# A reordered first ten microseconds: x tiles 4 and 5 load ahead of two weight remainders, x 1 on the sync queue, T2 one chunk earlier, and xT of tile 3 copied in halves

## The chip, the cores and the metric

One core of one Trainium2 chip. The metric is the device time of one execution in microseconds (us). Every execution told of here was in the fast state: the granted clock was 0.997 to 1.0 of full speed in all of them.

Positions such as "T2 at 7.38" are us from the first instruction of the profiled execution. PE is TensorE's matmul, PEld its weight load, DVE VectorE, ACT ScalarE, POOL GpSimd, SP SyncE (which issues most DMA loads). PSUM is the memory into which PE writes. T0, T1 and so on are the four transposes of that tile of x; K0, Q0, H4 and the like are accumulations of matmuls, each in one bank.

## The reference, cut to what matters

```python
x  = A_x                                  # [1, 2048, 448] bf16
xn = _layernorm(x, axis=-1)
s  = _A_ref(xn, A_wqkv, A_wo)             # linear attention: 16 heads of 28, phi(t) = t+1 or exp(t)
g  = _silu(_B_ref(xn, B_w1, B_b1, B_w2, B_b2))   # FFN 448 -> 1792 -> 448, squared ReLU
return x + s * g
```

Only the beginning matters: x is normalized per token (DVE), transposed (PE, via PSUM), and multiplied by wqkv and w1. 448 columns are three contraction chunks of 128 rows and a remainder of 64 rows.

## The kernel before

The program is written op by op in Python and put in order per engine; the first ~9 us, "the head", are laid out by hand. The loads go out in this order (cut):

```python
load_x(0, 1)
load_x(1, 2, "act").prio = -118                     # x tile 1: issued by ScalarE
twins = load_k("sp", w_qkv, A_wqkv, "wk", 384, 2 * D, later=True)   # "wk": the K part of wqkv
load_x(2, 4)
# ... b1 on ScalarE's queue ...
load_w1("w1a", 0, 512, 2, [twins])                  # two main loads, then twins, then the 64-row remainders
load_x(4, 8)
load_w1("w1b", 512, 1024)
load_k("sp", w_qkv, A_wqkv, "wq", 0, 384)
load_w1("w1c", 1024, F)
```

A DMA issued from SP occupies SP while it is issued, and SP issues one after the other. The last loads of `load_w1` are the 64-row remainders of w1 ("w1 rests" below for those of w1a).

A tile of x becomes normalized (`ln_norm`, columns 0 to 383), then its last 64 columns are written twice into columns 384 to 511 (`ln_last`, the "twin", so that 64-row matmuls can run in pairs on both halves of the array). Then four 128x128 transposes go into one PSUM bank and one copy takes them to xT:

```python
def pe_transpose(si, part, eng):
    b = Buf("T")                                    # a PSUM bank of its own
    chunks = range(4) if part is None else (2 * part, 2 * part + 1)
    # ... one transpose per chunk into b; the fourth reads the twin ("xd") ...
    if eng == "dve":
        return e.tensor_copy(dst, src)
    return e.activation(out=dst, in_=src, func=AF.Copy)
```

PE's order in the head (cut); `first` and `second` are the two token halves of the first four h (= w1) accumulations:

```python
turn(0, 0, "act"); turn(0, 1, "act"); turn(1, 0, "act")    # T0, first half of T1
mains(k0, (0,), ...); mains(k0, (1,), ...); mains(k0, (2,), ...)   # K of tile 0
turn(1, 1, "act")
mains(k1, (0, 1), ...); h_mains(0, (0, 1)); mains(k1, (2,), ...)
# ... b1 transpose ...
h_mains(0, (2,)); h_mains(1); h_mains(2)
head["xT2"] = pe_transpose(2, None, "act")                 # T2
h_mains(3)
head["xT3"] = pe_transpose(3, None, "dve")                 # T3
rests(k0, k1)                                              # 64-row remainders of K
rests(first[0], first[2]); rests(first[1], first[3])       # 64-row remainders of h: need the w1 rests
pe_four(*second)                                           # second halves of h: need xT of tiles 2 and 3
# then K2 H4 K3 H6, H5 Q0 Q1 H7 H8 ...                     # H4 on needs w1b, H8 on needs w1c
```

## Time and profile before

| | before |
|---|---|
| time, median of 3 (range) | 141.42 us (141.3 to 141.51) |
| span of the profiled execution | 139.7 us |
| PE busy | 136.6 us (98%) |
| T2 starts, second half of h starts, K2 starts | 7.38, 8.84, 10.38 us |
| landed: wk, x 2 and 3, w1 rests, last of w1b, last of w1c | 4.07, 4.73, 7.03, 10.51, 15.38 us |

From the page of the profile of before: the span, each engine's busy time, and by engine the chain of work that ended last.

```profile
span 139.7 us, 3106 instructions
...
PE 136.6 (98%) x1255; PEld 68.0 (49%) x1255; DVE 92.2 (66%) x226; ACT 77.8 (56%) x152; POOL 25.0 (18%) x33
...
PE 95%; DVE 2%; DMA 2%; issue 0%; DVEq 0%
```

TensorE is the limit nearly everywhere. So the change can only win or lose time in which PE stands still or runs slowly in the head. PE's timeline there (start, duration, engine, line, operation, out<-in, shapes, count; an idle time before it would follow in brackets):

```profile
4.92 0.81 PE L641 MATMUL pb<-w_qkv,xT 128*128 128x512 bf16 x3
...
6.60 0.93 PE L688 MATMUL pb<-xT,w 128*128 128x256 bf16 x7
7.38 0.40 PE L528 MATMUL pb<-ident,xn 128*128 128x128 bf16 x4
7.61 0.49 PE L688 MATMUL pb<-xT,w 128*128 128x256 bf16 x3
7.94 0.39 PE L528 MATMUL pb<-ident,xn 128*128 128x128 bf16 x4
8.26 0.39 PE L641 MATMUL pb<-w_qkv,xT 64*128 64x512 bf16 x2
8.48 1.30 PE L688 MATMUL pb<-xT,w 64*128 64x256 bf16 x18
...
10.38 1.03 PE L641 MATMUL pb<-w_qkv,xT 64*128 64x512 bf16 x8
```

The first line is K0, the last K2; the L528 lines are T2 and T3. The view merges both halves of h into the line of 8.48; the weight loads (PEld) show where the second half starts:

```profile
8.84 1.42 PEld L688 LDWEIGHTS pb<-xT,w 64*128 64x128 bf16 x28 [0.26 <-DVE xT L537]
```

A matmul's shown duration includes its latency, so compare starts: seven h matmuls fill 6.60 to 7.38, about 0.11 us each. DVE's timeline in the same execution:

```profile
5.10 0.62 DVE L463 BATCH_NORM_STATS2 st<-x_tok 128x6 f32<-128x448 bf16 x1
...
6.94 0.37 DVE L486 TENSOR_SCALAR xn<-x_tok,mv,rstd 128x384 bf16<-128x384 bf16 x1
7.26 0.31 DVE L512 TENSOR_SCALAR xn<-x_tok,mv,rstd 128x128 bf16<-128x128 bf16 x1
...
8.36 0.42 DVE L537 COPY xT<-pb 128x512 bf16<-128x512 bf16 x1 [0.49 <-PE pb L528]
```

The statistics of x 2 ("st2" below) start at 5.10 without a wait, as x 2 and 3 landed at 4.73. xn of tile 2 is done at 7.31, 0.07 before PE comes to T2. The copy of xT 3 ends at 8.78, and the second half of h starts right after it, at 8.84. And the loads as SP issues them (duration: of issuing, not of moving data):

```profile
0.44 0.42 SPq L401 DMA_DIRECT2D w_qkv<-in_A_wqkv_dram  x1
0.91 0.49 SPq L401 DMA_DIRECT2D x_tok<-in_A_x_dram  x1
...
3.68 1.24 SPq L401 DMA_DIRECT2D w<-in_B_w_dram  x2
4.96 0.59 SPq L401 DMA_DIRECT2D x_tok<-in_A_x_dram  x1
5.58 1.62 SPq L401 DMA_DIRECT2D w<-in_B_w_dram  x3
...
9.06 1.77 SPq L401 DMA_DIRECT2D w<-in_B_w_dram  x3
```

In this order: wk, x 2 and 3, the w1 rests, x 4 to 7, w1b, w1c. One issue takes 0.4 to 0.6 us, and SP is never idle.

### The profile page before, as it was taken

The page shows a single profiled execution, that of the slowest core. Times are in us where ns is not written, and L with a number is a line of the kernel's source. Part 1 is how long each engine was busy: PE and PEld are TensorE (multiplying, and loading weights), DVE is VectorE, ACT ScalarE, POOL GpSimd, SP SyncE. Part 2 cuts the span into 40 slices and gives each one's busy share as a digit, 9 for nine tenths or more (in the row PEclk, how much of TensorE's full clock was granted, in tenths as well). Part 3 has the DMA queues.
Part 4 walks back from the last instruction along what each step waited for, and adds up shares of the span by engine and source line. Part 5 has one row for each costly group of instructions (what it writes and reads, how often), then busy time and mean ns, then how long its engine had stood idle before and what let it go on. Part 6 is the DMA issues. An engine that isn't in the chain of part 4 may idle for free.

```text
span 139.7 us, 3106 instructions
## 1 busy us (share of the span) xinstructions
PE 136.6 (98%) x1255; PEld 68.0 (49%) x1255; DVE 92.2 (66%) x226; ACT 77.8 (56%) x152; POOL 25.0 (18%) x33
## 2 busy tenths in 40 slices
PE   9999999999999999999999999999999999999992
PEld 2474444444444444444455455645555555555481
DVE  3989899799878994889995900329636071542653
ACT  4769787879988878979788912422033030301220
POOL 6000000000000000000893000000002328091770
DMA  6997367999723200000000148960000103111122
GB/s 190 247 335 219 77 170 186 356 276 144 131 52 70 60 6 0 0 19 5 0 0 0 42 120 169 175 107 0 0 0 5 66 0 101 35 66 66 38 99 68
DMA packets 20354, 12.91 MB, mean 92 GB/s; under 512 B 9524, under 2 KB 19956, under 8 KB 20340
## 3 DMA queue, kind: packets, MB, share of 16 engines
q1 hardware_dynamic: 18332, 11.52, 33.3%
q10 hardware_dynamic: 2008, 1.20, 4.3%
q8 instruction: 10, 0.16, 0.5%
q14 instruction: 4, 0.03, 0.1%
HBM read 8.78 MB, written 2.10 MB: 78 GB/s over the span
## 4 chain that ended last, share of the span: by engine, by line
PE 95%; DVE 2%; DMA 2%; issue 0%; DVEq 0%
PE pb L955 31%; PE pb L688 30%; PE pb L641 9%; PE pb L1021 8%; PE pb L722 7%; PE pb L672 6%; DMA x_tok<-in_A_x_dram 2%; PE pb L528 1%; PE pb L728 1%; DVE st L463 1%; PE pb L815 1%; PE pb L776 1%; PE pb L853 0%; DVE xn L991 0%; DVE mv L464 0%; PE pb L846 0%
## 5 line engine op out<-in xcount | busy, mean ns | idle before, releaser
L688 PE MATMUL pb<-xT,w 64*128 64x512 bf16 (+2 forms) x408 | 51.6, 365 | 0.0
L955 PE MATMUL pb<-w,r 64*128 64x448 bf16 (+3 forms) x406 | 44.9, 343 | 0.0
L697 ACT ACTIVATE r<-pb,b1f 128x512 bf16<-128x512 f32 x56 | 35.1, 688 | 4.2 <-PE pb L688 4.2
L688 PEld LDWEIGHTS pb<-xT,w 64*128 64x128 bf16 (+1 forms) x408 | 22.8, 94 | 22.5 <-ACT r L697 0.5
L955 PEld LDWEIGHTS pb<-w,r 64*128 64x128 bf16 (+1 forms) x406 | 22.8, 95 | 19.9 <-issue 0.7
L966 DVE TENSOR_TENSOR gbuf<-pb,b2b 128x448 bf16<-128x448 f32 (+1 forms) x16 | 9.2, 608 | 30.0 <-PE pb L955 30.0
L931 ACT ACTIVATE gbuf<-gbuf 128x448 bf16<-128x448 bf16 (+1 forms) x16 | 8.7, 565 | 36.0 <-DVE gbuf L966 35.5
L1000 POOL TENSOR_TENSOR xn<-xn,x_tok 128x448 bf16<-128x448 bf16 x15 | 15.0, 1032 | 46.3 <-DVE xn L991 46.3
L641 PE MATMUL pb<-w_qkv,xT 64*128 64x512 bf16 (+1 forms) x106 | 17.8, 376 | 0.0
L672 PE MATMUL pb<-xT,w_qkv 64*128 64x512 bf16 x84 | 15.5, 376 | 0.0
L705 DVE TENSOR_TENSOR r<-r 128x512 bf16<-128x512 bf16 x42 | 14.4, 418 | 0.0
L390 POOL MEMSET kvm<- 128x2048 bf16 x1 | 1.8, 1804 | 63.4 <-DVE zb L666 63.4
L1021 PE MATMUL pb<-msb,pqT 64*128 64x448 bf16 (+3 forms) x93 | 10.9, 343 | 0.0
L629 DVE SCALAR_TENSOR_TENSOR qk<-pb,qk 128x512 bf16<-128x512 f32 x16 | 10.6, 685 | 0.2
L463 DVE BATCH_NORM_STATS2 st<-x_tok 128x6 f32<-128x448 bf16 x16 | 9.3, 610 | 2.0 <-DMA x_tok<-in_A_x_dram 2.0
L991 DVE TENSOR_TENSOR xn<-pb,gbuf 128x448 bf16<-128x448 f32 (+2 forms) x17 | 9.2, 591 | 2.0 <-ACT gbuf L931 1.5
L619 ACT ACTIVATE qk<-pb 128x512 bf16<-128x512 f32 x16 | 8.9, 593 | 3.0 <-PE pb L641 2.5
L641 PEld LDWEIGHTS pb<-w_qkv,xT 64*128 64x128 bf16 (+1 forms) x106 | 6.7, 94 | 6.0 <-ACT xT L538 0.2
L722 PE MATMUL pb<-qk,xn 128*128 128x448 bf16 x48 | 9.3, 353 | 0.0
L619 ACT ACTIVATE pqT<-pb 128x512 bf16<-128x512 f32 x12 | 6.8, 597 | 3.2 <-PE pb L688 1.6
L672 PEld LDWEIGHTS pb<-xT,w_qkv 64*128 64x128 bf16 x84 | 6.0, 94 | 5.0
L706 ACT ACTIVATE r<-r 128x512 bf16<-128x512 bf16 x14 | 8.4, 637 | 0.0
(71 smaller groups left out, 99.7 us busy)
## 6 DMA issues: line engine op xcount, KB each, us to landing
out_dram<-xn SPq DMA_DIRECT2D x15, 112.0 KB, 1.7
w<-in_B_w_dram SPq DMA_DIRECT2D x1, 1568.0 KB, 10.0
x_tok<-in_A_x_dram SPq DMA_DIRECT2D x3, 448.0 KB, 3.8
xT<-rows ACTq DMA_DIRECT2D x6, 112.0 KB
w<-in_B_w_dram SPq DMA_DIRECT2D x1, 576.0 KB, 4.6
xT<-rows SPq DMA_DIRECT2D x5, 112.0 KB
w_o<-in_A_wo_dram SPq DMA_DIRECT2D x1, 392.0 KB, 11.3
w_qkv<-in_A_wqkv_dram SPq DMA_DIRECT2D x1, 384.0 KB, 3.6
```

The costliest lines, as they stand in the source:

```text
L463: add("dve", lambda e, _: e.bn_stats(st6[:, si, :], x_tok[:, si, :]), [("x", si)], [("st", si)], 0.58),
L619: add("act", lambda e, _: e.activation(out=slot, in_=src(), func=AF.Exp), [buf, "actw"], [tile], 0.6)
L629: lambda e, _: e.scalar_tensor_tensor(out=slot, in0=src(), scalar=1.0 + 1e-6, in1=slot, op0=ALU.add, op1=ALU.max),
L641: return e.matmul(ps(b)[:, 0:512], xT[half[h], c, si * P : (si + 1) * P], w_qkv[half[h], c, 384 : 2 * D], start=start, stop=stop,)
L672: return e.matmul(ps(b)[:, 0:512], w_qkv[half[h], c, m * P : (m + 1) * P], xT[half[h], c, g * 512 : (g + 1) * 512], start=start, stop=stop,)
L688: return e.matmul(ps(b)[:, c0 : c0 + n], w_1[half[h], c, fi * P : (fi + 1) * P], xT[half[h], c, t : t + n], start=start, stop=stop,)
L697: lambda e, _: e.activation(out=slot, in_=ps(b)[:, 0:512], func=AF.Relu, bias=b1f[:, fi : fi + 1]),
L705: return e.tensor_tensor(out=slot, in0=slot, in1=slot, op=ALU.mult)
L722: last = e.matmul(ps(b)[:, 0:D], xn[:, si, c * P : (c + 1) * P], pk_of(si), start=(si == 0), stop=(si == NT - 1),)
L955: return e.matmul(ps(b)[:, 0:n], r2[half[h], fi, si * P : (si + 1) * P], w_2[half[h], fi, c], start=start, stop=stop)
L1000: eng, lambda e, _: e.tensor_tensor(out=ob, in0=ob, in1=x_tok[:, si, c], op=ALU.add),
L1021: return e.matmul(ps(b)[:, 0:n], q, m, start=start, stop=stop)
```

## The change

The intent: shorten the wait at 8.84 (both engines copy half of xT 3 at the same time), give x 4 and 5 to DVE earlier, free ScalarE's queue at the start, shorten the twin's write, and let T2 and K0 start sooner. The diff, cut to its core:

```diff
         load_x(0, 1)
-        load_x(1, 2, "act").prio = -118
+        load_x(1, 2)
 # ...
-        load_w1("w1a", 0, 512, 2, [twins])
-        load_x(4, 8)
+        load_w1("w1a", 0, 512, 2, [twins, lambda: load_x(4, 6)])
+        load_x(6, 8)
 # ... ln_norm: all 448 columns also for tiles 1 to 3 (was 384)
-            twin = head[f"xd{i}"] = ln_last(i)
+            twin = head[f"xd{i}"] = ln_twin(i, i + 1, "dve") if i else ln_last(i)
 # ...
         warm(8, wide=True)
+        warm(2)
 # ...
+        mains(k0, (0,), [("xT", 0, "a")] + wnames("wk")[:1])
         turn(1, 0, "act")
-        mains(k0, (0,), [("xT", 0, "a")] + wnames("wk")[:1])
 # ...
         h_mains(1)
+        head["xT2"] = pe_transpose(2, None, "act")
         h_mains(2)
-        head["xT2"] = pe_transpose(2, None, "act")
         h_mains(3)
-        head["xT3"] = pe_transpose(3, None, "dve")
+        turn(3, 0, "dve")
+        turn(3, 1, "act")
 # ... DVE's order in the head: xn2 xd2 xn3 xd3 xT30 (was xd2 xn2 xd3 xn3 xT3); ScalarE's ends with xT31
```

`ln_twin` is a copy of 64 columns of xn, and depends on `ln_norm`; `ln_last` computed both twins anew from x.

More of the change, by code (lines that the diff above doesn't have):

```diff
@@ L482, in ln_norm @@
         def ln_norm(si, part=None):
-            c = (slice(0, D if si > 3 else 384), slice(0, 256), slice(256, 384))[0 if part is None else part + 1]
+            c = (slice(0, D), slice(0, 256), slice(256, D if si else 384))[0 if part is None else part + 1]
             return add(
@@ L1108, in bass_recurrent_scan__linear_attn_block__dense_activation_squared_relu__prompt_kernel @@
         for eng, names in (
-            ("dve", "st0 mv0 st1 mv1 xn00 xn01 xd0 xn10 xn11 xd1 st2 mv2 st3 mv3 xd2 xn2 xd3 xn3 xT3"),
-            ("act", "ln0 ex0 ln1 ex1 xT00a xT00 xT01 xT10 xT11 ln2 ex2 ln3 ex3 b1 xT2"),
+            ("dve", "st0 mv0 st1 mv1 xn00 xn01 xd0 xn10 xn11 xd1 st2 mv2 st3 mv3 xn2 xd2 xn3 xd3 xT30"),
+            ("act", "ln0 ex0 ln1 ex1 xT00a xT00 xT01 xT10 xT11 ln2 ex2 ln3 ex3 b1 xT2 xT31"),
         ):
@@ L1116, in bass_recurrent_scan__linear_attn_block__dense_activation_squared_relu__prompt_kernel @@
         for op in early:
-            op.after = [head["xT3" if op.eng == "dve" else "xT2"]]
+            op.after = [head["xT30" if op.eng == "dve" else "xT31"]]
         pe_four(*second)
@@ L1143, in bass_recurrent_scan__linear_attn_block__dense_activation_squared_relu__prompt_kernel @@
                         if op.writes[0][0] == "st":
-                            op.after = [head["xT3"]]
+                            op.after = [head["xT30"]]
             quads(g, first)
```

## The prediction

> **What bounds the kernel.** TensorE. The busy shares give PE 136.6 of 139.7 us; the chain of waits is 95% PE, unbroken from 4.1 us to 137 us. The change touches only the head (0 to 9 us), so it can gain only PE idle time there. From single instructions of the timeline: the first transpose starts at 4.09; six transposes up to 4.87 hold about 0.4 us of waits for DVE's xn; from 4.92 on matmuls follow at their issue rate (0.215 us per 512 columns, 0.108 per 256) except about 0.1 us before the first 64-row remainders (8.16 to 8.26) and about 0.15 us at 8.84, where the second half of h waits for DVE's 0.42 us copy of xT 3 (8.36 to 8.78; the waits view lists 0.26 of weight-load idle). So the stall aimed at is 0.15 us, 0.1% of the time; everything in the head is under 0.8 us, 0.6%.
>
> **What the change does.**
> 1. Copy of xT 3 in halves: DVE 0.42 becomes about 0.3 (256 columns) beside ScalarE 0.38. ScalarE's half comes last: gain at best 0.1 us. ScalarE's first Exp of K (8.69) moves to about 8.8; harmless.
> 2. Twin: per tile a 0.31 us tensor_scalar (0.22 start to start) becomes a dependent 64-column copy (estimate 0.15, from 0.20 for 128 columns at 13.37); xn grows to 448 columns at almost no cost. xn 2 would be ready near 7.1 rather than 7.32, xn 3 near 7.6 rather than 7.87, the twins only about 0.05 earlier.
> 3. T2 ahead of the third h chunk: it would start at about 7.1, but its fourth transpose waits for the twin (7.3). PE does not reorder: the Trainium skill, "TensorE: Matmul & The Clock Gate", Part 2, says matmuls stay in order; the trace's starts agree (7.257 h, 7.375 T2, 7.608 h). So h pays a wait of 0.05 to 0.1 us there.
> 4. K 0 ahead of T1: delays T1's copy on ScalarE by 0.2 us, K 1 by about 0.05.
> 5. x 1 on the sync queue: each issue takes SyncE 0.39 to 0.6 us, so every later load is issued 0.45 us later. The skill, "DMA: Bandwidth & Descriptors", "Issuing engines are not separate DMA queues": another issuing engine saves only issue time. wk lands near 4.5 (was 4.07, needed 4.8); x 2, 3 near 5.1 (4.73; DVE wants it at 5.10, so up to 0.1 us of DVE wait); w1 rests near 8.1 (7.03, needed 8.4) as x 4, 5 now precede them.
> 6. Two more warm matmuls fill idle PE time before 4.09.
>
> Gains and losses nearly cancel: the second half of h starts at 8.6 to 9.0 (8.84). After it PE is the limit, so this shift is the whole difference; a changed later order of DVE and ScalarE may add 0.1.
>
> **Predicted:** 141.3 us, 8 times in 10 within 140.9 to 141.8. Faster by over 2%: 0.5%; within 2%: 98.5%; slower by over 2%: 1%.
>
> **Right if** PE busy stays 136 to 137 us, the PE idle at 8.84 shrinks but a wait on the twin appears near T2, ScalarE does half of xT 3, and K2 starts (before: 10.38) within 0.25 us of that.
>
> **Wrong if** the w1 rests land after 8.4 or w1b after 11.0 (was 10.5) and PE stands still; if x 2, 3 delays DVE's chain by 0.3 us; if PE's full clock comes a window later (transposes take 0.29 us up to 4.53, 0.22 from 4.87); or if a changed order of DVE and ScalarE adds stalls after 9 us.

## The result, and the profile after

| | before | after |
|---|---|---|
| time, median of 6 (range) | 141.47 us (141.3 to 141.86) | 141.91 us (141.46 to 142.0) |
| ratio, 95% interval | | 1.0024 (1.0006 to 1.0042) |
| span of the profiled execution | 139.7 us | 140.5 us |
| T2, second half of h, K2 start | 7.38, 8.84, 10.38 | 7.82, 9.72, 11.26 |
| K2's start to the end | 129.27 | 129.28 |
| landed: wk, x 2 and 3, w1 rests, w1b, w1c | 4.07, 4.73, 7.03, 10.51, 15.38 | 4.89, 5.55, 8.53, 11.14, 16.55 |

A ratio here and below is the mean time of one kernel's fast runs over that of the other's of the same rounds, so it isn't quite the ratio of the medians. The interval says slower, by 0.06 to 0.42%. The time predicted, 141.3, was 0.6 too low, and the range's upper end, 141.8, is 0.11 below the median.

One caution about the two profiles. The profiled execution of before was one of its quickest: its span, 139.7, is 0.2 shorter than the 139.9 of the execution timed at 141.34, and in every other run the time was about 1.4 us over the profile's span. So the two profiles differ by 0.9 us where the medians differ by 0.44; the pair shows where time can be lost, and the experiments must say how much of it is typical.

From the page of the profile of after:

```profile
span 140.5 us, 3109 instructions
...
PE 137.3 (98%) x1257; PEld 68.6 (49%) x1257; DVE 92.2 (66%) x226; ACT 78.4 (56%) x153; POOL 25.0 (18%) x33
...
PE 95%; DMA 3%; SPq 1%; DVE 0%; issue 0%; DVEq 0%
```

The last line is already a hint: the chain now begins with 3% of DMA and 1% of SP's issuing, where before it began with DVE and x. PE's timeline:

```profile
5.03 0.58 PE L641 MATMUL pb<-w_qkv,xT 128*128 128x512 bf16 x1 [0.30 <-DMA w_qkv<-in_A_wqkv_dram]
5.41 0.42 PE L528 MATMUL pb<-ident,xn 128*128 128x128 bf16 x2
...
7.25 0.60 PE L688 MATMUL pb<-xT,w 128*128 128x256 bf16 x4
7.82 0.45 PE L528 MATMUL pb<-ident,xn 128*128 128x128 bf16 x4
8.11 0.82 PE L688 MATMUL pb<-xT,w 128*128 128x256 bf16 x6
8.76 0.48 PE L528 MATMUL pb<-ident,xn 128*128 128x128 bf16 x4
9.18 0.39 PE L641 MATMUL pb<-w_qkv,xT 64*128 64x512 bf16 x2
...
11.26 1.03 PE L641 MATMUL pb<-w_qkv,xT 64*128 64x512 bf16 x8
```

Three things to see. K0 waited 0.30 us for wk, and T1 (5.41), whose data were ready by then, waited behind it. The Trainium skill, "TensorE: Matmul & The Clock Gate", Part 2, says that matmuls stay in program order and that only weight loads are pulled ahead; this trace agrees (T1 at 5.41 behind K0 at 5.03). Second, K0's 512 columns took 0.58 us: PE still ran at half rate, as it did in before's profile up to the transpose at 4.53 (0.29 us there, 0.22 from 4.87 on). In after full rate came at 6.00 only; by their starts, the four matmuls from 5.03 to 6.00 took 0.43 us more than they would have at full rate. Third, T2 starts at 7.82 although three h matmuls fewer precede it: the four of 7.25 were through by about 7.69. What it waited for is on DVE's timeline:

```profile
5.58 0.63 DVE L463 BATCH_NORM_STATS2 st<-x_tok 128x6 f32<-128x448 bf16 x1 [0.47 <-DMA x_tok<-in_A_x_dram]
...
7.37 0.40 DVE L486 TENSOR_SCALAR xn<-x_tok,mv,rstd 128x448 bf16<-128x448 bf16 x1 [0.22 <-ACT rstd L477]
7.80 0.18 DVE L501 COPY xn<-xn 128x64 bf16<-128x64 bf16 x1
...
9.07 0.29 DVE L537 COPY xT<-pb 128x256 bf16<-128x256 bf16 x1 [0.57 <-PE pb L528]
```

st2 waited 0.47 us for x 2 and 3, and the whole chain behind it is as much later: xn of tile 2 at 7.77 in place of 7.31. So PE was held at once by a late, slow start and by DVE's chain (7.69 against 7.77). The two are not independent: xn waited 0.22 for ScalarE's rstd, and ScalarE came to that step only behind its copy of T1's second half (6.53 to 6.92), which had waited for PE. Without this, xn would have been ready at about 7.58 (an estimate: the step before it on DVE ended at 7.15, then 0.03 from step to step and 0.40 for xn). ScalarE's half of xT 3:

```profile
9.28 0.39 ACT L538 ACTIVATE xT<-pb 128x256 bf16<-128x256 bf16 x1 [0.38 <-PE pb L528]
```

and the weight loads of the second half of h behind it:

```profile
9.72 1.42 PEld L688 LDWEIGHTS pb<-xT,w 64*128 64x128 bf16 x28 [0.21 <-ACT xT L538]
```

The halves take 0.29 and 0.39, and as predicted ScalarE's ends last; the second half of h starts at 9.72. And SP's issues:

```profile
0.92 0.43 SPq L401 DMA_DIRECT2D w_qkv<-in_A_wqkv_dram  x1
1.39 0.49 SPq L401 DMA_DIRECT2D x_tok<-in_A_x_dram  x1
...
4.16 0.58 SPq L401 DMA_DIRECT2D x_tok<-in_A_x_dram  x1
4.79 1.10 SPq L401 DMA_DIRECT2D w<-in_B_w_dram  x2
5.93 0.58 SPq L401 DMA_DIRECT2D x_tok<-in_A_x_dram  x1
6.56 1.61 SPq L401 DMA_DIRECT2D w<-in_B_w_dram  x3
...
10.03 0.59 SPq L401 DMA_DIRECT2D w<-in_B_w_dram  x1
```

wk and x 2 and 3 are issued 0.48 later, w1b and w1c 0.97 later (6.56 against 5.58, 10.03 against 9.06), because there are two more issues and not one. But wk and x 2 and 3 landed 0.82 later, that is 0.34 more than they were issued later. The windows view (us, busy time of PE, PEld, DVE, ACT, POOL with counts, PE's clock, DMA's share, GB/s) shows a slow spell. Before:

```profile
2.20:3.20 1.00, 1.00 (x3) 0.30 (x2) 0.94 (x3) 0.10 (x1) 0.80 (x4) 1.00 0.96 289
```

And the same window of after:

```profile
2.20:3.20 1.00, 1.00 (x3) 0.30 (x2) 0.96 (x3) 0.19 (x1) 0.79 (x4) 1.00 0.92 122
```

The 16 DMA engines were busy for 0.92 of that microsecond in after, yet moved less than half as much. From 3.2 to 5.0 us both move 350 to 370 GB/s. The same window in all 20 profiles: the ten with x 1 on SP moved 122 to 187 GB/s in it, the ten with x 1 on ScalarE's queue 281 to 349. (The clock column shows 1.00 in both although PE ran at half rate there; for the warm-up one has to look at durations.)

### The profile page after: what moved, and what is told of

It is laid out like the page before. It is cut to its first block, busy times and chain, and to the rows that moved or that the text cites. A ratio compares the mean times of both kernels' runs of the same rounds, so it can differ in the third digit from the quotient of the medians.

```text
span 140.5 us, 3109 instructions
## 1 busy us (share of the span) xinstructions
PE 137.3 (98%) x1257; PEld 68.6 (49%) x1257; DVE 92.2 (66%) x226; ACT 78.4 (56%) x153; POOL 25.0 (18%) x33
## 4 chain that ended last, share of the span: by engine, by line
PE 95%; DMA 3%; SPq 1%; DVE 0%; issue 0%; DVEq 0%
PE pb L955 30%; PE pb L688 30%; PE pb L641 9%; PE pb L1021 8%; PE pb L722 7%; PE pb L672 6%; DMA w_qkv<-in_A_wqkv_dram 3%; PE pb L728 1%; PE pb L815 1%; PE pb L528 1%; PE pb L776 1%; SPq L401 1%; PE pb L853 0%; DVE xn L991 0%; PE pb L846 0%
## 5 line engine op out<-in xcount | busy, mean ns | idle before, releaser
L641 PE MATMUL pb<-w_qkv,xT 64*128 64x512 bf16 (+1 forms) x106 | 18.4, 380 | 0.3 <-DMA w_qkv<-in_A_wqkv_dram 0.3
```

The source lines that it names most:

```text
L641: return e.matmul(ps(b)[:, 0:512], xT[half[h], c, si * P : (si + 1) * P], w_qkv[half[h], c, 384 : 2 * D], start=start, stop=stop,)
```

## The experiments

Two theories at the start. L, loads: x 1 on SP delays wk and x 2 and 3, and that alone is the loss; put x 1 back and it is gone. O, order: what is lost lies in the new order of PE, DVE and ScalarE, loads or no. Of the parts, five can be taken alone: x 1's queue, x 4 and 5's place, T2's place, the halves, K0's place. Runs 1 to 4, 5 to 8, 9 to 12, 13 to 16 and 17 to 18 each shared a chip and the runs of before. "Before" in these five calls had medians of 141.39, 141.43, 141.34, 141.34 and 141.44. The expectations count the runs in this order.

### 1. After, x 1 back on ScalarE's queue

```diff
-        load_x(1, 2)
+        load_x(1, 2, "act").prio = -118
```

> The kernel after, with x 1 put back on ScalarE's queue; all else as after. Theory L (loads): x 1 on the sync queue issues every later load 0.47 us later and makes wk and x 2, 3 land 0.82 us later, and the head loses about 0.8 us of the profile by it. Then here wk lands by 4.2 us and x 2, 3 by 4.8 (after: 4.89, 5.55), the second half of h starts at 8.6 to 8.9 (9.72), and the time is 141.2 to 141.5 us. Rival C (clock): matmuls ran at half rate up to 5.6 us in the profile of after, up to 4.5 in that of before, and it is the late full clock, brought by the new order of PE's head, that costs; then the slow matmuls stay here up to 5.6 and the time stays near 141.8. Rival R (order): T2 ahead of the third h chunk and K 0 ahead of T1 stall PE by themselves; then the time falls only half way, to about 141.7.

Measured: 141.67 (141.35 to 141.94), ratio 1.0013 (0.9992 to 1.0033). In its profile, 141.94, wk landed at 4.17 but x 2 and 3 at 5.77 and the w1 rests at 8.87; T2 started at 7.81 and K2 at 11.25, as in after. So theory L did not get its clear win. The profile also shows that x 2 and 3 can straggle with x 1 on ScalarE's queue. And PE's full rate came as late as in after, at 5.97, as the rival C of the expectation (the clock) had it for the profile; see "A part that is scatter" below.

### 2. Before, x 1 on SP

```diff
-        load_x(1, 2, "act").prio = -118
+        load_x(1, 2)
```

> The kernel before, with x 1 alone moved to the sync queue. Theory L: wk lands at about 4.9 us, x 2, 3 at about 5.5, DVE waits 0.4 us or more for x 2, and the time is 141.7 to 142.0 us, most of the loss or all of it. Rivals C and R: 141.4 to 141.6, as the order of PE's head is that of before.

Measured: 141.5 (141.39 to 141.84), ratio 1.0003 (0.9984 to 1.0022). wk 4.44, x 2 and 3 5.09, w1 rests 7.58: all later by about 0.4 to 0.5, T2 at 7.30, K2 at 10.40. Up to K2 the later loads cost nothing here: 5.09 is just when DVE comes to st2. Behind it, H4 started 0.23 late, at 11.50 (the last of w1b landed at 11.24). Theory L, as stated, falls: the loss needs something more than x 1's queue.

### 3. After, T2 back behind the third h chunk

```diff
-        head["xT2"] = pe_transpose(2, None, "act")
         h_mains(2)
+        head["xT2"] = pe_transpose(2, None, "act")
```

> The kernel after, with T2 back behind the third h chunk, x 1 still on the sync queue. Theory L with its second step (with x 2, 3 late, PE waits at T2 for DVE's xn while the three matmuls of the third h chunk, 0.33 us, could have run): the second half of h starts 0.15 to 0.2 us sooner than the 9.72 of after, the time is 141.7 to 141.8 us. Rival R: 141.5 or less. Rival C: no change, 141.9.

Measured: 141.65 (141.34 to 142.24), ratio 1.0012 (0.9987 to 1.0038): between the two, not resolved from either. Its profile shows something that neither theory had: the second and the third of T3's four transposes, between which the halves part, start at 8.38 and 8.85, 0.47 apart in place of the usual 0.06. The next run shows why.

### 4. After, x 1 on ScalarE's queue and T2 back

The edits of 1 and 3 together.

> The kernel after, with x 1 on ScalarE's queue and T2 back behind the third h chunk. Theory L: x 2, 3 is in time, so the place of T2 matters little: within 0.1 us of the first run of this call, 141.2 to 141.5 us, with the second half of h at 8.65 to 8.9. Rival R: clearly faster than the first run of this call, by 0.15 us or more.

Measured: 141.73 (141.69 to 142.28), ratio 1.0024 (1.0004 to 1.0045). wk landed at 4.00 and x 2 and 3 at 4.67, as in before, and it is still slower. PE's timeline in its profile:

```profile
7.53 0.39 PE L528 MATMUL pb<-ident,xn 128*128 128x128 bf16 x4
...
8.09 0.28 PE L528 MATMUL pb<-ident,xn 128*128 128x128 bf16 x2
8.61 0.29 PE L528 MATMUL pb<-ident,xn 128*128 128x128 bf16 x2 [0.25 <-ACT xT L538]
```

and ScalarE's:

```profile
7.96 0.60 ACT L538 ACTIVATE xT<-pb 128x512 bf16<-128x512 bf16 x1 [0.53 <-PE pb L528]
```

The second half of T3 waits until ScalarE has copied xT of tile 2 (8.56). That is a wait for a PSUM bank: K0, K1, four of h, T2 and the first half of T3 are eight, and the second half takes T2's bank. A whole T3 in one bank does not need a ninth. In after the same wait exists, but T2 was moved forward and its copy ends at 8.90, so only 0.09 is left. So "T2 first" is what makes the halves affordable, and taking T2 back alone was no clean experiment for O. The prediction had not counted banks. (Both halves in one bank would be no way out: the Trainium skill, "PSUM — Partial Sum Buffer", "PSUM bank collisions raise a hardware error", says that DVE and ScalarE may not read one bank at once; no run here tries it.)

### 5. Before, with the halves

```diff
-        head["xT3"] = pe_transpose(3, None, "dve")
+        turn(3, 0, "dve")
+        turn(3, 1, "act")
 # and the names xT30, xT31 in the orders of DVE and ScalarE
```

> The kernel before, with the copy of xT 3 in halves alone. Theory B (banks): the head has no free PSUM bank there (K 0, K 1 and four h hold six, T2 and the first half of T3 the other two), so the second half of T3 has to wait until ScalarE has copied T2; in the fourth run of the first call this put 0.47 us between the halves of T3. Then here 0.3 to 0.5 us lie between the second and the third transpose of T3, the second half of h starts at 9.1 to 9.4 (before: 8.84), and the lowest time is over 141.5 us, the median 141.6 to 141.9. Rival: halving only shortens the copy, as the change means it: 8.7 to 8.8 and at most 141.4.

Measured: 141.93 (141.49 to 142.16), ratio 1.0029 (1.0008 to 1.0049). The second and third transposes of T3 start at 8.71 and 9.18: again 0.47 apart. The halves alone cost about 0.4 to 0.5 us, more than the 0.1 that they were to win.

### 6. Before, K0's first matmul ahead of T1

```diff
-        turn(1, 0, "act")
         mains(k0, (0,), [("xT", 0, "a")] + wnames("wk")[:1])
+        turn(1, 0, "act")
```

> The kernel before, with the first matmul of K 0 ahead of the first half of T1 alone. Theory O (order): T1 now stands behind a matmul that waits for wk and for the first copy of xT 0; ScalarE's copy of T1 then starts 0.2 us later and K 1 up to 0.1 us: K 1 starts at 5.75 to 5.85 (before: 5.68) when wk is in time, and the median is within 0.15 us of before. Were this the main cost of the change: 141.7 or more.

Measured: 141.44 (141.27 to 143.04), ratio 1.0014 (0.9979 to 1.005). K1 started at 5.81 in place of 5.68, K2 at 10.51. With wk in time (4.20) K0's place costs 0.1 at most in the profile, and nothing that the times resolve.

### 7. After, K0 back behind T1

The reverse edit, on after.

> The kernel after, with T1 back ahead of the first matmul of K 0. Theory O joined with the late wk (4.4 to 4.9 us where x 1 is on the sync queue): T1 no longer waits for wk, so the head gains 0.1 to 0.4 us on after: 141.5 to 141.75. If only banks and the twin cost: 141.8 to 141.9, as after.

Measured: 141.76 (141.36 to 142.73), ratio 1.0023 (0.9994 to 1.0052); the profiled execution, 141.41, was a quick one: wk 4.48, x 2 and 3 5.15, T2 7.30, K2 10.73. Its transposes of T2 wait 0.13 for xn and 0.04 for the twin, T3's second half 0.09 for its bank, the second half of h 0.1. These sum to 0.36, with the loads nearly in time; 0.1 ahead of the rests comes on top, as in before, which had 0.25 in all (0.1 ahead of the rests, 0.15 at 8.84).

### 8. After, xT 3 copied whole by DVE

The reverse of 5, on after.

> The kernel after, with the copy of xT 3 whole on DVE again. Theory B: with T2 ahead of the third h chunk its bank is free nearly in time (0.09 us between the halves of T3 in the profile of after), so halving costs little there and gains what it was meant to gain, about 0.1: time 141.8 to 142.0, as after or a little above, with the second half of h waiting 0.15 to 0.25 us for DVE. If halving is what costs in after too: 141.5.

Measured: 141.78 (141.38 to 142.21), ratio 1.0023 (1.0 to 1.0046). In the profiled execution (141.47) T2 was early, 7.02, and PE ran into another wait:

```profile
8.27 0.39 PE L641 MATMUL pb<-w_qkv,xT 64*128 64x512 bf16 x2
9.09 1.16 PE L688 MATMUL pb<-xT,w 64*128 64x256 bf16 x18 [0.43 <-DMA w<-in_B_w_dram]
```

The w1 rests landed at 9.04, and PE wanted them at about 8.49. This is the first run in which the place of x 4 and 5, ahead of the rests, is seen to cost: the prediction had 8.1 for that landing.

### 9. Before, x 4 and 5 ahead of the w1 rests

```diff
-        load_w1("w1a", 0, 512, 2, [twins])
-        load_x(4, 8)
+        load_w1("w1a", 0, 512, 2, [twins, lambda: load_x(4, 6)])
+        load_x(6, 8)
```

> The kernel before, with x 4, 5 loaded ahead of the h remainders alone. Theory W (w1 remainders): they are issued one load later, land at 7.6 to 8.4 us (before: 7.03) and are wanted at 8.48; so PE mostly does not wait yet, and waits up to 0.3 us where a load straggles: median 141.4 to 141.7, w1 remainders landing 0.6 to 1.3 later than before. Rival: the order of loads is free, as before to 0.05 us.

Measured: 141.42 (141.07 to 141.88), ratio 1.0 (0.9975 to 1.0025). The rests landed at 7.74, w1c at 15.6. With x 1 on ScalarE's queue and before's order, x 4 and 5 can go first at no cost that the times resolve (the interval reaches to 0.25%).

### 10. After, x 4 to 7 in one load behind the rests again

The reverse edit, on after.

> The kernel after, with the h remainders ahead of x 4 to 7 again, x 1 still on the sync queue. Theory W: where PE and DVE are in time, PE stood still 0.43 us for the remainders in the eighth run (landed 9.04, wanted 8.49); with them ahead they land by 7.8, and the quick executions get quicker: lowest time 141.2 to 141.4, median 141.5 to 141.75. If only banks, twin and order count: as after, median 141.8 to 141.9.

Measured: 141.44 (141.29 to 141.77), ratio 1.0002 (0.9981 to 1.0023). One part undone, and the kernel is as fast as before. The profiled execution (141.29): wk 4.33, x 2 and 3 4.97, rests 7.32, T2 7.14, K2 10.57.

### 11. Before, with the copied twin, and T3 ahead of the last h matmul

```diff
 # the twin as in the change, then:
-        h_mains(3)
+        h_mains(3, (0, 1))
         head["xT3"] = pe_transpose(3, None, "dve")
+        h_mains(3, (2,))
```

> A trial for a better kernel: the kernel before with the twin as a copy, and T3 ahead of the last matmul of the fourth h chunk, its copy whole on DVE; loads, T2, K 0 and banks as before. xn 3 is ready near 7.65, so T3 starts at 7.8 without a wait and DVE's copy is over at 8.7: the second half of h starts at 8.68 to 8.75 (before: 8.84) with no wait for DVE. Time 0.1 us below before: 141.3, not to be told from before by the times. If the twin costs by itself (its dependent copy), 141.5 or more.

This is the version that the findings pointed to: keep before's loads, banks and whole copy; use the cheaper twin; and put a matmul that is ready between T3 and the wait for its copy. Measured: 141.2 (141.04 to 141.47), ratio 0.9985 (0.9964 to 1.0006). PE's timeline:

```profile
7.66 0.38 PE L688 MATMUL pb<-xT,w 128*128 128x256 bf16 x2
7.88 0.39 PE L528 MATMUL pb<-ident,xn 128*128 128x128 bf16 x4
8.11 0.27 PE L688 MATMUL pb<-xT,w 128*128 128x256 bf16 x1
```

Run 18 repeats it.

### 12. After, again

No edit.

> The kernel after once more, to see how far its times and the start of its head scatter. If the shift is its own: median 141.7 to 141.95, 0.25 to 0.45 above before; the full clock (last half-rate matmul, 5.6 us in the first profile) and the landing of x 2, 3 (5.55) may lie elsewhere, by 1 us and 0.5 us, as they did between the eight runs so far. If the first profile's late clock made the loss: a profile with full clock before 4.8 goes with 141.5 or less.

Measured: 141.95 (141.15 to 142.11), ratio 1.0021 (0.9993 to 1.0049). The result repeats, but one of its executions took 141.15. In the profiled one, 142.11, x 2 and 3 landed at 5.46, and further on PE waited once more:

```profile
12.34 1.02 PE L688 MATMUL pb<-xT,w 64*128 64x512 bf16 x7 [0.30 <-ACT vep L473]
```

This is H4. The releaser named, ScalarE's vep (a step of the layer norm), is not the cause: the last remainder of w1b landed at 12.11 by its semaphore, and H4's matmuls need it. So a late w1b can cost too. It was issued at the same time as in the first profile of after (from 6.56 on), where its last part landed at 11.14, so its later issue is at most part of the cause.

### 13. Before, x 4 to 7 in one load, ahead of the rests

```diff
-        load_w1("w1a", 0, 512, 2, [twins])
-        load_x(4, 8)
+        load_w1("w1a", 0, 512, 2, [twins, lambda: load_x(4, 8)])
```

> The kernel before with all of x 4 to 7 (448 KB) ahead of the h remainders: the suspected delay doubled, all else as before. Theory W: the remainders land at 8.6 to 9.3 us, wanted at 8.48; PE stands still for them 0.2 to 0.7 us in the profile and the median is 141.6 to 142.0. If their landing does not matter: 141.3 to 141.45.

Measured: 141.48 (141.26 to 143.33), ratio 1.0028 (0.9989 to 1.0067): the interval holds 1, so neither a loss nor its absence is shown. The median expected if the landing mattered, 141.6 to 142.0, was not reached. The rests landed at 8.83 and PE's weight load waited 0.28 for them in the profile (141.59): twice the bytes ahead of the rests bring them somewhat too late even with x 1 on ScalarE's queue; w1c landed at 15.04.

### 14. After, both load changes undone

The edits of 1 and 10 together.

> The kernel after with both changes of the loads undone (x 1 on ScalarE's queue, remainders ahead of x 4 to 7); the order of PE, DVE and ScalarE as in after. Theory W: 141.35 to 141.5, as the tenth run; what is left over before (bank 0.09, T2's wait for xn and twin about 0.15, less 0.05 of the last wait) is about 0.1 to 0.2 us, and the second half of h starts at 8.9 to 9.05. If the order on the engines is what costs: 141.7 or more.

Measured: 141.6 (141.37 to 142.11), ratio 1.0019 (1.0002 to 1.0035). Better than after's 141.9, but not before. In the profiled execution (141.6) wk came at 3.78, x 2 and 3 straggled to 5.53, and T2 started at 7.56, K2 at 10.94. The interval just leaves out 1, so what is left when both load changes are undone, the order on the engines, seems to cost something: 0.26 us by these medians, of one call.

### 15. Run 10 again

> The tenth run's kernel again (after, remainders ahead of x 4 to 7). If its 141.44 was its own: median 141.35 to 141.6. If it was luck: 141.7 to 141.95.

Measured: 141.57 (141.35 to 142.12), ratio 1.0017 (1.0001 to 1.0033). wk 4.50, x 2 and 3 5.15, T2 7.21, K2 10.64. Run 10's full recovery was partly luck; the two together (12 executions) have a median of 141.51, with 1 at 141.8 or more.

### 16. After, a third time

> The kernel after a third time. As twice before: median 141.8 to 142.0. If in this profile the full clock, wk and x 2, 3 come early (by 4.6, 4.5 and 5.1 us), theory W says that PE now waits for the remainders, which land at 8.5 to 9.0, after it wants them at about 8.5 to 8.7.

Measured: 141.98 (141.1 to 142.47), ratio 1.0039 (1.0013 to 1.0065). wk 4.93, x 2 and 3 5.51, PE waited 0.34 for wk, T2 7.59, K2 11.02. H8 started 0.24 late, at 17.31: the last of w1c landed at 17.11. In three profiles of after, wk has now landed at 4.89, 4.82 and 4.93, and in the six other profiles so far of kernels with x 1 on SP (runs 2, 3, 7, 8, 10, 15) from 4.33 to 4.50.

### 17. After, in another memory layout

To see whether that 0.4 is an accident of where things lie in memory: an unused internal tensor of 1 MB in front, and one POOL memset more at the end, so that addresses and code move; nothing in the head changes.

```diff
+        pad_d = nc.dram_tensor("pad", [P, 4096], bf, kind="Internal").ap()
         rows_d = nc.dram_tensor("rows", [P, 512], bf, kind="Internal").ap()
 # and one memset of msz twice, late in the program
```

> The kernel after with one unused internal DRAM tensor of 1 MB and one more memset on POOL near 60 us: the order on PE, DVE, ScalarE and SyncE is that of after, only the layout in memory can differ. If after's late wk hangs on its layout: wk lands by 4.5 us, x 2, 3 by 5.15, median 141.5 to 141.75. If it belongs to the order of instructions as such: wk at 4.8 to 4.95, median 141.85 to 142.0. If it is scatter: one of the two, which this run can't tell from the first.

Measured: 141.9 (141.5 to 142.91), ratio 1.0026 (1.0006 to 1.0046): the same slowness. But in its profile wk landed at 4.50 and x 2 and 3 at 5.26, and K2 started at 10.63. So the later landing does not come in every execution of this order, and an execution can be slow without it; what made the other five slow can't be seen. The profiled one, 142.91, lost its time elsewhere:

```profile
16.46 0.38 PE L672 MATMUL pb<-xT,w_qkv 64*128 64x512 bf16 x1
18.36 0.37 PE L688 MATMUL pb<-xT,w 64*128 64x512 bf16 x1 [1.52 <-ACT r L697]
```

This is H8, which needs w1c. The releaser named is again ScalarE, but the last part of w1c landed at 18.16 by its semaphore and PE's wait in its queue ended at 18.19. In before w1c landed at 15.38.

### 18. Run 11 again

> The eleventh run's kernel again (before with the twin as a copy and T3 ahead of the last matmul of the fourth h chunk). The head gains 0.05 to 0.1 us by its profile (second half of h at 8.79 with T 0 at 4.16, where before had 8.84 with T 0 at 4.09): 0.05 to 0.2 us below before by the times. If the first result was luck with the clock: within 0.05 of before or above it.

Measured: 141.28 (141.07 to 141.63), ratio 0.999 (0.9973 to 1.0006). The profiled execution, 141.63, was its slowest, with 0.23 lost to a DMA transpose at 22.9. Twice this version had a median 0.14 to 0.16 below before's of the same call, and its 12 executions all stayed under 141.7, while 7 of 61 of before's reached 141.8; but both intervals hold 1. A gain of 0.1% is likely and not shown.

### The profiles side by side

Landings and starts in us; "time" is that of the profiled execution.

| kernel | time | wk | x 2,3 | w1 rests | w1c | T2 | K2 | K2 to end |
|---|---|---|---|---|---|---|---|---|
| before | (span 139.7) | 4.07 | 4.73 | 7.03 | 15.38 | 7.38 | 10.38 | 129.27 |
| 2 before, x 1 on SP | 141.39 | 4.44 | 5.09 | 7.58 | 15.35 | 7.30 | 10.40 | 129.56 |
| 5 before, halves | 142.16 | 3.84 | 5.13 | 7.38 | 14.78 | 8.09 | 11.48 | 129.28 |
| 9 before, x 4,5 first | 141.14 | 3.79 | 4.58 | 7.74 | 15.6 | 7.35 | 10.36 | 129.35 |
| 11 before, twin, T3 inside | 141.29 | 3.90 | 4.56 | 7.05 | 14.89 | 7.44 | 10.33 | 129.55 |
| after | 141.94 | 4.89 | 5.55 | 8.53 | 16.55 | 7.82 | 11.26 | 129.28 |
| 12 after again | 142.11 | 4.82 | 5.46 | 8.74 | 16.9 | 7.58 | 11.02 | 129.69 |
| 16 after, third | 141.93 | 4.93 | 5.51 | 8.32 | 17.11 | 7.59 | 11.02 | 129.47 |
| 17 after, other layout | 142.91 | 4.50 | 5.26 | 8.26 | 18.16 | 7.20 | 10.63 | 130.88 |
| 10 after, x 4..7 back | 141.29 | 4.33 | 4.97 | 7.32 | 15.59 | 7.14 | 10.57 | 129.33 |
| 15 the same again | 141.57 | 4.50 | 5.15 | 7.67 | 14.78 | 7.21 | 10.64 | 129.53 |
| 14 after, loads back | 141.6 | 3.78 | 5.53 | 7.92 | 15.08 | 7.56 | 10.94 | 129.26 |

## Why the prediction was right or wrong

**Right: what bounds the kernel, and the size of the stakes.** PE busy was 137.3 of 140.5 us, slightly over the 136 to 137 of the prediction. Everything from K2 on took 129.27 and 129.28 us in the pair, so that pair's difference lies wholly in the head (run 17 lost 1.5 us behind it), and "within 2%", given 98.5%, holds. The halves' durations (0.29 and 0.39, predicted 0.3 and 0.38) and the rule that PE does not reorder were right as well.

**Wrong: step 5, the sync queue's delay, mis-sized.** The prediction wrote "every later load is issued 0.45 us later. ... wk lands near 4.5 (was 4.07, needed 4.8); x 2, 3 near 5.1 (...up to 0.1 us of DVE wait); w1 rests near 8.1". Measured: 4.89, 5.55 with 0.47 of DVE wait, and 8.53. Two terms of that sum were off.

- One issue was not counted. x 4 to 7 had been one load, and in two it costs SP a second issue of ~0.6 us. SP issued the w1b and w1c loads 0.97 later, not 0.45. What came late was then waited for in some execution at each place: the w1 rests (run 8, 0.43 us), w1b (run 12, 0.30), w1c (run 16, about 0.24, and run 17, 1.52). Kernels with both the split and x 1 on SP landed w1c at 15.91 to 18.16 in seven profiles; those with x 4 to 7 in one load at 14.78 to 15.59 in ten; those with the split and x 1 on ScalarE's queue at 15.6 to 16.7 in three. The issues are not all of it: in the first seven w1c was issued at 10.02 to 10.04 every time, and its landing still scattered over 2.25 us.
- wk and x 2 and 3 landed 0.34 later than their later issue explains, with the slow spell of the DMA at 2.2 to 3.2 us (122 against 289 GB/s). Runs 2 and 10, with x 1 on SP too, had 176 and 187 GB/s there and landed wk at 4.44 and 4.33. The spell comes with x 1 on SP, but it is not shown to cause the 0.34: run 3 had 133 GB/s and landed wk at 4.42, x 2 and 3 at 5.07. This is the term that the pair's profile shows as lost time: PE waited 0.30 for wk and DVE 0.47 for x 2 and 3. The Trainium skill, "DMA: Bandwidth & Descriptors", "Issuing engines are not separate DMA queues", on which this step rested, says that another issuing engine saves only issue time, "usually small relative to the DMA itself". Here that time was 0.48 us, on loads with 0.4 to 0.7 us of slack, and the 0.34 came on top.

**How the lateness becomes time.** The prediction had listed these risks under "Wrong if" (x 2 and 3 delaying DVE's chain by 0.3, a late full clock, w1 rests after 8.4 with PE standing still), but as unlikely. What it did not see is how the change ties T2 to them. In the ten profiles with T2 first, T2 follows st2's start by 1.92 to 2.24 us: in after (5.58 and 7.82), run 12 (5.48 and 7.58) and run 10 (5.03 and 7.14), for instance. In after DVE was ready for st2 at 5.10, so x 2 and 3 later than that are lost nearly one for one. At the same time K0, now ahead of T1, holds up PE when wk is late. In after both limits lay within 0.1 us (PE 7.69, 0.43 of it by the half rate; DVE 7.77, 0.19 of it by PE through ScalarE), in run 12 too (7.56 and 7.52). This fits that undoing one of the parts x 1, T2, K0 or the halves alone did little (runs 1, 3, 7, 8: 24 executions, median 141.75), and that x 1 on SP, x 4 and 5 first, or K0 first cost nothing that the times resolve when done alone on before (runs 2, 9, 6). It does not explain run 10, where undoing one part did nearly all.

**Wrong: "gains and losses nearly cancel" in steps 1 to 4.** Step 1's gain of "at best 0.1" for the halves missed the PSUM bank: a wait of 0.41 us in runs 3, 4 and 5 (0.47 from start to start, less the usual 0.06), 0.09 in after, where T2 goes first. Step 3 had T2 "at about 7.1" with 0.05 to 0.1 of wait; with loads in time it was 7.14 (run 10), and the twin's wait 0.04 (run 7), so this was right, but T2 first brings no gain in its turn: from T2 to K2 it took 3.43 to 3.44 us in after and in runs 10, 12, 15, 16 and 17, against 3.01 in before with three matmuls (0.33 us, by their starts) fewer. So the new order costs about 0.10 there, the bank's 0.09 for the most part. Step 4's "+0.05" for K1 was 0.13 in run 6, where T0 itself started 0.05 later (4.14). The twin's copy took 0.18, the estimate was 0.15.

**How much each is worth, and how surely.** After: 18 executions, median 141.94, 14 of them at 141.8 or more. Before: 61 executions, median 141.39, 7 at 141.8 or more. With x 4 to 7 back in one load behind the rests (runs 10 and 15): 141.51, 1 of 12. So by the times the place and the split of that load, together with x 1 on SP, carry most of the half microsecond. How is not shown. That load is issued at 4.16, behind wk and x 2 and 3 (0.92 and 1.39), so it cannot have delayed their issue, yet in runs 10 and 15 these landed earlier too; and in the three profiles of after PE never waited for the rests (landed at 8.32 to 8.74, wanted at about 9.2 to 9.4). What the load can have delayed, w1b or w1c, PE waited for in runs 12, 16 and 17, and not in runs 10 and 15. No run splits the load without moving it, or moves it unsplit on after. The rest, 0.1 to 0.25 us, would be the order on the engines (0.12 by runs 10 and 15 together, 0.26 by run 14, and the 0.10 above). The larger part rests on the times of two runs of one kernel against three of another, whose intervals overlap; on the counts at 141.8 (1 of 12 against 14 of 18) they do not look alike.

**A part that is scatter, and a rival.** The position of the first full-rate matmul ranged from 3.1 (run 8) to about 6 us (run 5, between 5.9 and 6.3) over the 20 profiles. The Trainium skill, "TensorE: Matmul & The Clock Gate", Part 1, has a free-running window of about 3.4 us that must be busy before the clock doubles; a spread of about 3 us agrees with that. Run 5's profile and after's both fell late in it, those of runs 1, 12 and 16 too (5.97, 5.55 and 5.44). Of the six profiles with full rate after 5.2 (these and run 7's) five are of executions of 141.9 us or more, of the other fourteen three. So all three profiles of after had a late full rate, and it is a rival for part of what they show. It is not enough for T2: in runs 12 and 16 DVE had xn of tile 2 at 7.52 and 7.53, against 7.31 in before, with at most 0.04 of waiting for ScalarE before it, so by x 2 and 3. After's one profile with an early full rate (run 17, 3.64) had x 2 and 3 earlier as well, and K2 at 10.63; no run separates the two.

**Open.** By what way the load of x 4 and 5 costs time. Why wk and x 2 and 3 came in 0.3 to 0.4 later in all three profiles of after than in the other kernels with x 1 on SP; run 17 neither confirmed the layout nor excluded chance. And whether the slow timed executions of after mostly lost their time to the late head or to the late w1 parts: only the profiled ones can be looked into, and they show both.

## What to carry to other kernels

Before adding or splitting a load on a queue that is never idle, count the issues ahead of every later load and compare each landing with the moment its first reader wants it, down to the last load, not just the next two. Before splitting a PSUM eviction over two engines, count the banks: the second half may wait for the very copy it was to run beside. And when two limits lie within 0.1 us of each other, undoing one part can show little; undo them in pairs too, and repeat the best one, since here the best one (run 10) was 0.51 us below after in its call and its repeat (run 15) 0.41.

## What the Trainium skill lacked or had wrong

- "DMA: Bandwidth & Descriptors", "Issuing engines are not separate DMA queues": "usually small relative to the DMA itself" holds for one load here (0.42 of 3.6 us for wk), but that section has no warning that issues add up on a queue without idle time ("Perfetto Trace Analysis", "Optimizing DMA Performance", does name the issuing engine's sequencer as a possible limit). One issue took 0.39 to 0.6 us here; two more ahead of them put the issue of w1b and w1c off by 0.97 us, and w1c landed at 15.91 to 18.16 in the seven profiles of such kernels, in before's at 15.38 (how much of that is scatter is open).
- On no page did I find the slow spell of the first loads: at 2.2 to 3.2 us the DMA engines moved 122 to 187 GB/s in the ten profiles with x 1 on SP, 281 to 349 in the ten with x 1 on ScalarE's queue. Of the trace's DMA packets in that window, 9 to 21 took 0.25 us or longer with x 1 on SP, 1 to 3 with x 1 on ScalarE's queue.
- On no page did I find how far the landing of one load scatters: x 2 and 3, issued at 0.91 to 0.92 us, landed from 4.56 to 5.77 in ten profiles, and issued at 1.38 to 1.39 from 4.97 to 5.55 in the ten others.
- "TensorE: Matmul & The Clock Gate", Part 1: the transition is given as varying by "±500ns run-to-run"; it varied from 3.1 to about 6 us here, over twenty profiles of related kernels, which fits the same page's free-running window but not that figure. A note in the same part, that one kernel had 6, 11 or 14 slow matmuls in different runs, is nearer to it. The profile's clock column stayed at 1.00 while 512 columns took 0.58 us in place of 0.38, so durations show the warm-up and that column doesn't.
- "Perfetto Trace Analysis", "Identifying Dependency Chains", notes that an instruction that waits on several engines may have EventSemaphore instructions ahead of it, and the traces show these here. On no page did I find that the releaser a profile view names can then be the wrong one: twice (runs 12 and 17; 0.30 and 1.52 us) the one named was a ScalarE instruction, while a DMA's semaphore, at 12.11 and 18.16, was the last to come.
